# Gates of a recurrent attention kernel in two passes, and weight bits by ACT: one predicted change

## The chip, the cores and the metric

The kernel runs on one core of a Trainium2 chip. Time is the device time of one execution, in microseconds (us); the kernel before was run three times, with a median of 344.8 us (344.57 to 345.37). One further execution was recorded by the hardware profiler, and all rows of a trace come from it. The engines are PE (TensorE, matrix products, with its separate weight load PEld), DVE (VectorE), ACT (ScalarE), POOL (GpSimd) and SP (SyncE, which here only issues transfers). Each engine works through its own list of instructions in order, and waits where an instruction's operands are not there yet. ACT and POOL issue transfers too.

## The reference

The first part is a recurrent attention (an mLSTM) over 4 batches, 8 heads, 768 steps of 40 values. Each head keeps a matrix C and a vector n, and two gates per step, stabilized by a running maximum m:

```python
for t in range(S):
    m_new = np.maximum(f_gate[:, :, t] + m, i_gate[:, :, t])
    f_stab = np.exp(f_gate[:, :, t] + m - m_new)
    i_stab = np.exp(i_gate[:, :, t] - m_new)
    m = m_new
    C = f_stab[..., None, None] * C + i_stab[..., None, None] * (v_t outer k_t)
    n = f_stab[..., None] * n + i_stab[..., None] * k_t
    y[:, :, t] = sigmoid(o_gate[:, :, t]) * (C @ q_t) / max(abs(n . q_t), 1)
```

(The outer product and the dot products are written in short.) The second part takes y as x, 4 batches of 768 rows of 320: h = relu(x @ w_in) with 1024 columns is cut in u and v; v is normalized over its 512 columns; v_s = w_spatial @ v_n + b_spatial mixes the 768 rows of a batch; the output is (u * v_s) @ w_out. The weights w_in and w_out arrive as float64, all else as float32.

## The kernel before

**Blocks.** The recurrence is cut into 24 blocks n of 128 steps, six for each batch, all eight heads at once; a block has two chunks of 64 steps. A block's work is a chain over the engines:

- `s` on PE, the scores of the two chunks (L638); `ex` on PE (L641), which multiplies two small tables GM and AT and so gives the exponent of every gate weight; `W` on ACT (L656), its exponential; `KS` on DVE (L662), two products of scores and weights.
- `q` on POOL or DVE (L671), queries times the decay `Eb`. In the first batch Eb comes out of a product with `sel` (L651) and an exponential (L654); later batches load it from DRAM (L625).
- `kt` on POOL or DVE (L682), keys times weights in the tile RH; `dc` on PE (L693 for one chunk, L695 for the other), what each chunk adds to the state; the decays d1 and d2 of the state on POOL or DVE (L713, L723); the new states into RH on DVE (L716, L726), or for a batch's first chunk a copy.
- `pv` on PE (L737, L738), the outputs of scores and state; the denominators `den`, with ACT's part at L762 in the first batch, and `xm` (L753) and `xg` on DVE; the transposes `px` on PE (L786), and xH and xL, high and low halves of x.

Then `V` on PE (L839, tile pm) gives v of 128 rows, with its normalization on ACT, DVE and POOL; `pu` (L900) gives u; `pb` (L906 to L908) is the mixing over a batch's six blocks; g, gu, gh and gl on DVE and ACT make the gated product; `pc` (L950 to L952) is the output product, which is cast and stored. A float32 operand of these products is split into a high and a low part (H and L in the names) and three products of them are summed.

**Gates.** The gate rows are 32 (batch and head) by 768 steps. They are worked in three pieces, steps 0 to 128, 128 to 384 and 384 to 768: on DVE the running maximum m, a scan (L373), a difference (L380), its clipped negative (L383), a second scan that is reset at each chunk (L386) and a last difference (L389), for the two exponents g and a; then high parts on ACT (L407, L414) and low parts on DVE or POOL (L410, L417). The first piece goes by small transfers straight into GM and AT of block 0 (L447, L453). All pieces go into scratch in DRAM, from which SP loads each block's GM (L617) and each batch's AT (L464). ACT exponentiates g too (L428), and that scratch serves Eb.

**Weights.** w_in comes in five loads of float64 words and w_out in four. Each is turned into float32 by bits: ACT rebases the exponent of the upper word (L482, into wi_b or wir_b) and puts the sign into one byte in four of the tile sg (L486); DVE shifts the former left by three and joins the latter (L490), then joins the three top bits of the lower word (L493). A cast and a subtraction (L507) make the high and low parts.

**Order.** Two tables written out by hand set all of it: ORDER lists every task in the order in which it is emitted, for all engines together, and ENGINES names the engine of those tasks that have a choice. Two tasks joined by + are emitted in turns, instruction by instruction, as in `s2+dc1`. Tiles come from small pools, whose slots are reused in the order of the table.

Of the kernel before, what the change touches and what calls it, by code (L numbers as in the profile page):

```python
# [8 lines left out]
F32 = mybir.dt.float32  # L9
# [3 lines left out]
F8 = mybir.dt.float8e5  # L13
AF = mybir.ActivationFunctionType
# [22 lines left out]
PIECES = ((0, 128), (128, 384), (384, 768))  # L37
# [83 lines left out]
kt1 s2+dc1 d1_1 wi10_l0 ks1_1 q1_1 c1_1 qk3 wg0 wir_m0 gm4 wi01_0 W2 ko3 ra1 wir_m1 px0 wi01_1 xh0 ws04_l ws02_h pv1 eg2 wi01_2 ebm3 xl0 xj0 xk0 ks2_1
ws05_ld wir_m2 ex3 d2_1 q2_0 V00 gm5 ws02_l kt2 c2_1 ks2_0 da_1 Eb3 dp_1 xm1 xg1 we2 wi00_1 eg1 wi00_0 eg0 wi01_5 wi00_2 dc2+s3 W3 wi00_5 px1 d1_2
c1_2 re00 pv2 sq00 th2 ks3_1 wi01_h0 ws05_h xj1 q3_1 q3_0 d2_2 c2_2 ko4 kt3 d1_3 qk4 da_2 va00 wi01_l0 ks3_0 ex4 po00 dc3 c1_3 xh1 ebm4 Eb4 qk5 wo2_ld
ws05_l d2_3 dp_2 pv3 xk1 xm2 W4 kt4 xg2 xl1 ebm5 th3 da_3 ws00_ld c2_3 nb00 ex5 q4_0 dp_3 px2 xh2 Eb5 xj2 vn00 th4 W5 we0 gm6 xm3 xg3 xl2 s4 ks4_0
ks4_1 V01 dc4+s5 re01 ko5 sq01 px3 d1_4 xk2 c1_4 q4_1 pv4 ks5_0 wi00_h0 xh3 wo2_0 gm7 da_4 q5_0 ks5_1 q5_1 va01 dp_4 xj3 vh00 ws00_h d2_4 we1 c2_4 V02
re02 kt5 ex6 W6 xm4 ko6 d1_5 dc5 xg4 sq02 px4 ws00_l c1_5 po01 kt6 xh4 xj4 nb01 vh01 xk4 xl3 vl00 va02 po02 qk6 xl4 wi00_l0 vn01 pv5 eb7_0 eb6_0 qk7
da_5 dc6+s6 c1_6 th5 nb02 vn02 ko7 th6 vl01 eb7_1 V04 vh02 xk3 ks6_0 d2_6 re04 wir_z1 dp_5 V03 q6_1 q7_1 wo2_1 sq04 xm5 xg5 px5 ex7 s7 ws11_ld gm8
re03 ks6_1 wo2_2 va04 vl02 wo2_5 po04 pv6 W7 kt7 ks7_0 xj5 sq03 nb04 vn04 xh5 c2_6 vh04 xk5 xl5 q7_0 pu000 ex8 va03 ws03_ld ws11_h ws03_h vl04 po03
dc7 den6 ks7_1 V05 W8 ws01_ld d1_7 ws01_h qk8 nb03 vh03 ws15_ld ra2 qk9 ws01_l ws11_l c1_7 ws03_l re05 eb8_1 u000 ws13_ld gm9 pu001 sq05 va05 wo1_ld
ws15_h po05 vn03 u001 xm6 vl03 pv7 s8 nb05 s9 vh05 ex9 ws12_ld vn05 bsp eb8_0 vl05 xg6 ws15_l pb001 ko8 wo3_ld ws13_h gm10 W9 ks9_0 ws12_h ks8_0 wo1_0  # L130
wo2_h0 ws13_l wo1_1 wo1_2 pb003 gm11 d2_7 q8_1 wo2_l0 wo1_5 g001 den7 wo1_h0 wo3_0 wo3_1 ks9_1 wo0_ld wo1_l0 ko9 c2_7 ks8_1 pu003 g003 eb9_1 th7 u003
wo3_2 wo3_5 gu001 wo0_1 q8_0 ws12_l kt8 xm7 px6 xh6 d1_8 wo3_h0 gh001 xg7 wo3_l0 gu003 gl001 pu011 ws14_ld pb000 ws14_h u011 wo0_0 wo0_2 dc8 wo0_5 kt9
dc9 q9_0 c1_8 pu002 g000 gu000 ws14_l eb9_0 d2_8 pb002 ko10 wo0_h0 u002 ws10_ld c2_8 d1_9 pv8 c1_9 wo0_l0 g002 gh003 gl003 eb11_1 th8 q9_1 ws10_h pv9
xl6 gu002 ws10_l ex10 W10 d2_9 gh000 gh002 gl000 den8 qk11 kt10 pu010 pb011 eb10_0 gl002 g011 xm8 c2_9 den9 eb10_1 th10 d1_10 gm12 c02 qk10 oc02 gu011
eb11_0 xg8 c01 xm9 oc01 q10_0 c00 q11_0 u010 s10+dc10 ko11 xj6 ks10_1 xk6 oc00 th9 ks10_0 s11 px8 xh8 q10_1 c1_10 d2_10 pb010 ex11 xg9 ko12 pv10 q11_1
xl8 xj8 xk8 g010 px9 den10 xm10 eb12_0 gh011 W11 ex12 W12 qk12 pb013 xg10 px10 gu010 gh010 ks11_1 ks11_0 xh9 ko13 xh10 xl10 c2_10 pb012 pu012 u012 xj9
# [61 lines left out]
class Kernel:  # L198
# [155 lines left out]
    def gates(self):  # L354
# [7 lines left out]
        for z, (lo, hi) in enumerate(PIECES):  # L362
# [667 lines left out]
```

## Time and profile before

| what | value |
|---|---|
| median of three runs | 344.8 us (344.57 to 345.37) |
| the profiled execution's own time | 344.69 us |
| its span, first to last instruction | 342.9 us |
| PE busy | 321.5 us, 94% of the span |
| DVE busy | 243.1 us, 71% |
| ACT busy | 140.2 us, 41% |
| POOL busy | 140.0 us, 41% |
| DMA, mean | 123 GB/s |
| granted TensorE clock, mean | 0.999 |

The profile's page gives busy times, a picture of the span in 40 slices (each digit a busy share in tenths), groups of like instructions and a chain of waits. A row of the timeline gives the start in us from the span's start, the length in us, the engine, the line (L12 is line 12 of the kernel), the operation, output and inputs with their shapes, and in brackets how long the engine had been idle and what ended it. A row of a group gives the line, the count, busy us and mean ns of one, and after the second bar the idle time of the engine just before such instructions. A row of the waits gives who waited for what: us in all, how often, the longest.

### The profile page before, as it was taken

To read this page: it belongs to the slowest core of one execution; us is meant where nothing else is said; L and a number is where in the kernel's file an instruction comes from. 1 tells how busy PE (TensorE), PEld (TensorE's weight loads), DVE (VectorE), ACT (ScalarE), POOL (GpSimd) and SP (SyncE) were. 2 spreads that over 40 slices of the span, in tenths; PEclk is the share of its full clock that TensorE was granted. 3 is DMA by queue.
4 is the path that set the end of the run, shared out by engine and by line. 5 is a ranking of instruction groups with operands and counts; after the bars stand their busy time and mean duration, and the time that the engine had idled before them with its cause. 6 is when DMAs were issued, how large, how long until landed. Compare 5 with 4: busy or idle time off the path is not lost.

```text
span 342.9 us, 9048 instructions
## 1 busy us (share of the span) xinstructions
PE 321.5 (94%) x3654; PEld 296.0 (86%) x3654; DVE 243.1 (71%) x559; ACT 140.2 (41%) x327; POOL 140.0 (41%) x163
## 2 busy tenths in 40 slices
PE   2298899999999999999999999999999999999996
PEld 2177577898999989898999988999999889999995
DVE  4999999989856767857686677758838677325172
ACT  3769579844321159613113146740220187111001
POOL 6479898676444324561023227673300053100000
PEclk9999999999999999999999999999999999999999
DMA  8796877665343752324505522525210000100002
GB/s 244 253 328 188 248 236 239 165 226 171 121 119 112 233 150 90 106 73 142 175 30 175 181 62 87 175 65 182 98 38 2 3 0 21 38 0 21 19 21 76
DMA packets 17217, 42.13 MB, mean 123 GB/s; under 512 B 3572, under 2 KB 8664, under 8 KB 17176
## 3 DMA queue, kind: packets, MB, share of 16 engines
q1 hardware_dynamic: 11080, 24.31, 23.1%
q10 hardware_dynamic: 3872, 9.39, 8.2%
q0 software_dynamic: 2224, 7.86, 7.1%
q8 instruction: 29, 0.48, 0.6%
q14 instruction: 12, 0.10, 0.1%
HBM read 37.11 MB, written 4.42 MB: 121 GB/s over the span
## 4 chain that ended last, share of the span: by engine, by line
PE 79%; DVE 7%; ACT 4%; DMA 3%; POOL 3%; issue 2%; ACTq 0%; POOLq 0%; DVEq 0%
PE pu L900 13%; PE pm L839 12%; PE pb L906 9%; PE pb L908 9%; PE pb L907 9%; PE pv L737 5%; PE s L638 4%; PE pc L950 4%; PE pc L951 4%; PE pc L952 4%; PE px L786 2%; DMA ident<-in_ident 1%; POOL KS L671 1%; PE dc L693 1%; DMA ws<-in_w_sp 1%
## 5 line engine op out<-in xcount | busy, mean ns | idle before, releaser
L906 PE MATMUL pb<-wsH,vH 128*128 128x384 f32 x192 | 65.8, 342 | 0.0
L908 PE MATMUL pb<-wsH,vL 128*128 128x384 f32 x192 | 64.8, 338 | 0.0
L907 PE MATMUL pb<-wsL,vH 128*128 128x384 f32 x192 | 64.7, 337 | 0.0
L671 POOL TENSOR_TENSOR KS<-QK,Eb 40x512 f32<-40x512 f32 (+1 forms) x35 | 45.5, 1302 | 5.0 <-DMA QK<-in_qk 2.0
L662 DVE TENSOR_TENSOR KS<-s,W 64x512 f32<-64x512 f32 x48 | 32.9, 686 | 9.7 <-PE s L638 9.0
L924 DVE TENSOR_TENSOR pb<-pb,bsp 128x384 f32<-128x384 f32 x32 | 17.6, 560 | 26.9 <-PE pb L908 26.9
L638 PE MATMUL s<-QK 40*64 40x64 f32 x768 | 30.0, 233 | 6.7 <-DMA QK<-in_qk 6.2
L906 PEld LDWEIGHTS pb<-wsH,vH 128*128 128x128 f32 x192 | 36.1, 188 | 0.2
L907 PEld LDWEIGHTS pb<-wsL,vH 128*128 128x128 f32 x192 | 36.1, 188 | 0.1
L908 PEld LDWEIGHTS pb<-wsH,vL 128*128 128x128 f32 x192 | 36.0, 188 | 0.0
L638 PEld LDWEIGHTS s<-QK 40*64 40x64 f32 x768 | 27.0, 145 | 10.0 <-DMA QK<-in_qk 6.2
L723 POOL TENSOR_TENSOR tb<-RH,Eb 40x328 f32<-40x328 f32 x18 | 13.8, 768 | 52.6 <-DVE RH L716 28.3
L900 PE MATMUL pu<-xH,wiH 128*128 128x384 f32 x96 | 33.1, 345 | 0.4 <-DVE KS L662 0.4
L900 PE MATMUL pu<-xH,wiL 128*128 128x384 f32 x96 | 32.4, 338 | 0.0
L737 PEld LDWEIGHTS pv<-RH,KS 128*64 128x64 f32 x384 | 25.4, 145 | 7.9 <-issue 2.4
L737 PE MATMUL pv<-RH,KS 128*64 128x41 f32 x384 | 27.7, 237 | 3.7 <-DVE RH L716 2.4
L855 POOL TENSOR_TENSOR st<-st,half_neg 128x1 f32<-128x1 f32 x24 | 14.8, 618 | 39.8 <-DVE st L852 39.6
L839 PE MATMUL pm<-wiH,xH 128*128 128x512 f32 x72 | 30.3, 421 | 0.3 <-ACT W L656 0.3
L950 PE MATMUL pc<-woH,gt 128*128 128x320 f32 x96 | 29.9, 311 | 0.0
L951 PE MATMUL pc<-woL,gt 128*128 128x320 f32 x96 | 29.5, 308 | 0.0
L952 PE MATMUL pc<-woH,gt 128*128 128x320 f32 x96 | 29.5, 308 | 0.0
L839 PE MATMUL pm<-wiL,xH 128*128 128x512 f32 x72 | 29.1, 404 | 0.0
(133 smaller groups left out, 797.5 us busy)
## 6 DMA issues: line engine op xcount, KB each, us to landing
RH<-in_ko SPq DMA_DIRECT2D x12, 648.0 KB
QK<-in_qk SPq DMA_DIRECT2D x16, 448.0 KB
RH<-in_ko ACTq DMA_DIRECT2D x6, 648.0 KB
RH<-in_ko POOLq DMA_DIRECT2D x6, 648.0 KB, 5.5
Eb<-scr_e SPq DMA_DIRECT2D x33, 80.0 KB
ws<-in_w_sp SPq DMA_DIRECT2D x10, 192.0 KB
out<-o SPq DMA_DIRECT2D x12, 160.0 KB
out<-o ACTq DMA_DIRECT2D x12, 160.0 KB
```

What stands on the lines that cost most here:

```text
L638: yield self.nc.tensor.matmul(o[64 - p0:128 - p0, h], q[p0:p0 + D, 0, h], q[p0:p0 + D, 1, h], start=True, stop=True)
L662: self.nc.vector.tensor_tensor(out=KS.t[r, e], in0=st()[r], in1=self.T(W)[r], op=ALU.mult)
L671: self.on(f"q{n}_{e}", "POOL").tensor_tensor(out=KS.t[r, e], in0=self.T(QK)[r, 1], in1=self.T(Eb)[r], op=ALU.mult)
L737: self.nc.tensor.matmul(o[64:128, h], ks[:, 1, h], v1[:, h], start=True, stop=True)
L839: self.nc.tensor.matmul(pmt(), l, r, start=i == 0, stop=i == len(terms) - 1)
L900: self.nc.tensor.matmul(put(), w, x, start=i == 0, stop=i == len(terms) - 1)
L906: self.nc.tensor.matmul(pbt(), vH[:, cd], wh[:, s], start=s == 0, stop=False)
L907: self.nc.tensor.matmul(pbt(), vH[:, cd], wl[:, s], start=False, stop=False)
L908: self.nc.tensor.matmul(pbt(), vL[:, cd], wh[:, s], start=False, stop=s == NB - 1)
L950: self.nc.tensor.matmul(pct(), gH[:, c], wh[:, d], start=d == 0, stop=False)
L951: self.nc.tensor.matmul(pct(), gH[:, c], wl[:, d], start=False, stop=False)
L952: self.nc.tensor.matmul(pct(), gL[:, c], wh[:, d], start=False, stop=d == 3)
```

## The change

**Gates.** The first pass takes steps 0 to 128 on 32 rows, as before. Then one scan of the maximum covers the other 640 steps. Four differences of 192 steps each then put the four quarters of the sequence onto four groups of 32 partitions, so that all 128 partitions hold 192 steps; the clipped negative, the reset scan, the last difference, the high and low parts and the exponential are done once on 128 by 192. This second pass computes the first block's steps again, for the scratch. The scratch is laid out by quarters: a load of Eb takes 40 partitions by 8 heads in runs of 64 values from 8 places, where its source was one run of 512. There is one write each to the scratch of g, a and Eb where there were three. The order of the rows of g in GM changes, and the constants atr and sel with it.

**Weights.** The low bits are no longer joined by DVE at L493. ACT reads the top byte of the lower word as an integer from 0 to 255, multiplies it by 7.49/255 and stores it, as an integer from 0 to 7, into another byte of sg. The shift then joins sign and low bits at once.

**Tables.** ORDER and ENGINES are new throughout; the diff shows their first lines only. The pairs joined by + were `s2+dc1 dc2+s3 dc4+s5 dc6+s6 s10+dc10 s12+dc11 s13+dc13 dc14+s15 dc15+s16 s17+dc17 s18+dc18 s19+dc19 s20+dc20 s21+dc21 s22+dc23 s23+dc22` and are now `dc2+s3 s5+dc5 s7+dc7 s11+dc10 dc11+s12 s13+dc13 dc14+s15 s16+dc16 s17+dc17 s19+dc19 s21+dc20 s23+dc23 s22+dc22`. From the scores on, line numbers are two higher (L638 is L640).

```diff
-PIECES = ((0, 128), (128, 384), (384, 768))
...
 ORDER = """
-gmr1 sgz rst half_neg f gmr0 i ident m0 is0 atr0 fs0 g0 as0 wi11_ld qk0 msk sel wir_ld wir_z0 ko0 atc0 gh0 atr1 dg0 ah0 atc1 wi11_0 gl0 al0 m1 is1 dg3
-da0 dg1 fs1 g1 wa0 as1 wi11_1 dg2 s0 da1 gh1 gmc0 m2 wi11_2 gl1 wir_1 wg1 ex0 is2 fs2 ah1 wir_0 wi10_ld al1 qk1 W0 wir_2 ebm0 Eb0 ko1 kt0 gmc1 th0 dc0
...
+atr0 wir_z0 msk sgz i f rst gmr1 ident wi11_ld m0 is0 qk0 fs0 g0 as0 wir_ld gmc0 gmc1 gh0 gl0 sel dg2 ah0 al0 ko0 dg3 wi11_1 wi11_5 atc0 da1 s0 m1 nd2
+nd1 nd0 nd3 fs1 g1 as1 gmr0 dg0 wi11_0 wi10_ld ko1 dg1 gh1 da0 qk1 ah1 wir_1 gl1 wi11_2 wi01_ld ex0 W0 wir_5 ws05_ld ebm0 Eb0 al1 wir_0 wg kt0 ks0_1
+ks0_0 wir_2 wa dc0 wi10_1 wi10_5 wi10_0 qz_0 q0_1 c1_0 pv0 da_0 gm2 gm1 ra0 wi10_2 ebm1 d2_0 ebm2 ex1 c2_0 dp_0 qk2 ws02_ld atr1 th0 wi10_h0 Eb1 ex2
...
-        self.scr_g = dram.tile([BH, NB, 4, L], F32, name="scr_g")
-        self.scr_e = dram.tile([2 * NB, BH, L], F32, name="scr_e")
-        self.scr_a = dram.tile([BH, 2, S], F32, name="scr_a")
+        self.scr_g = dram.tile([BH, 4, NB // 2, 2, L], F32, name="scr_g")
+        self.scr_e = dram.tile([BH, 4, NB // 2, L], F32, name="scr_e")
+        self.scr_a = dram.tile([BH, 4, 2, S // 4], F32, name="scr_a")
...
 
     def gates(self):
...
-        for z, (lo, hi) in enumerate(PIECES):
...
-                self.nc.vector.tensor_tensor_scan(out=p[:, s:hi], data0=i[:, s - 1:hi - 1], data1=f[:, s:hi], initial=first, op0=ALU.max, op1=ALU.add)
...
-            add(f"fs{z}", "DVE", dve(n), fstab, r=[(ft, P)], w=[(eg, P)])
...
+        add("m0", "DVE", 0.5, lambda: scan_p(0, 128), r=[(ft, 0), (it, 0)], w=[(mt, 0)], lock=True)
+        add("m1", "DVE", 0.14 + 2.2 * 640 / 960.0, lambda: scan_p(128, S), r=[(ft, 1), (it, 0), (it, 1), (mt, 0)], w=[(mt, 1)], lock=True)
...
+        SEG = S // 4
+        for z in range(2):
...
+                for q in range(4):
+                    def diff(q=q):
+                        c = slice(q * SEG, (q + 1) * SEG)
+                        self.nc.vector.tensor_tensor(out=self.T(sg)[q * BH:(q + 1) * BH, 0:SEG], in0=T(it)[:, c], in1=T(mt)[:, c], op=ALU.subtract)
...
+            def fstab(A=A, Bf=Bf):
+                self.nc.vector.tensor_scalar(out=Bf(), in0=A(), scalar1=-1.0, scalar2=0.0, op0=ALU.mult, op1=ALU.min)
...
+            def scan_g(Bf=Bf, C=C, rows=rows, n=n):
+                self.nc.vector.tensor_tensor_scan(out=C(), data0=F("rst").t[0:rows, 0:n], data1=Bf(), initial=0.0, op0=ALU.mult, op1=ALU.add)
...
+            def a_sub(A=A, C=C):
+                self.nc.vector.scalar_tensor_tensor(out=A(), in0=A(), scalar=0.0, in1=C(), op0=ALU.min, op1=ALU.subtract)
...
+            add("wg", "SP", 0.4, lambda: self.dma("SP")(out=self.scr_g.rearrange("b s j w t -> s b (j w t)"), in_=half(0)), r=parts[0], w=[F("scr_g")], size=8)
+            add("wa", "SP", 0.4, lambda: self.dma("SP")(out=self.scr_a.rearrange("b s w x -> s b (w x)"), in_=half(1)), r=parts[1], w=[F("scr_a")], size=8)
+            add("eg", "ACT", 0.4 + n / 1200.0, lambda: self.nc.scalar.activation(out=Bf(), in_=C(), func=AF.Exp), r=[kc], w=[kb], due=25.0)
+            add("we", "SP", 0.35, lambda: self.dma("SP")(out=self.scr_e.rearrange("b s j t -> s b (j t)"), in_=Bf()), r=[kb], w=[F("scr_e")], size=8, due=29.0)
...
+    def load_a(self, b):
+
+        AT = self.F(f"AT{b % 2}")
+
+        def load():
+            return self.nc.sync.dma_start(
+                out=AT.t[68:84].bitcast(F32).rearrange("r (s x) -> r s x", s=4), in_=self.scr_a[b * H:(b + 1) * H].rearrange("h s w x -> w h s x"))
+        self.add(f"ra{b}", "SP", 0.6, load, r=[self.F("scr_a")], w=[(AT, ("a", z, w)) for z in range(2) for w in range(2)], size=16)
...
         def low():
-            self.nc.vector.scalar_tensor_tensor(out=bt(), in0=W()[:, :, 0], scalar=29, in1=bt(), op0=ALU.logical_shift_right, op1=ALU.bitwise_or)
+
+            self.nc.scalar.activation(
+                out=sg.t[:, 0:n].bitcast(U8).rearrange("p (n w) -> p n w", w=4)[:, :, 0], in_=top(),
+                func=AF.Copy, scale=7.49 / 255.0)
+
+        def top():
+            return self.T(rb, [128, 2 * n], F32).bitcast(U8).rearrange("p (n w) -> p n w", w=8)[:, :, 3]
 
         add(name + "_ld", "SP", 0.45, load, w=[rb], size=n, alt=LOADS)
         add(name + "_1", "ACT", c_act, rebase, r=[rb], w=[bits])
-        add(name + "_0", "ACT", c_act, sign, r=[rb], w=[signs], after=self.sgz)
+        add(name + "_0", "ACT", c_act, sign, r=[rb], w=[(signs, 0)], after=self.sgz)
+        add(name + "_5", "ACT", c_act + 0.16, low, r=[rb], w=[(signs, 1)], after=self.sgz)
         add(name + "_2", "DVE", c_dve, shift, r=[signs], w=[bits])
-        add(name + "_5", "DVE", c_dve, low, r=[rb], w=[bits])
...
-                        out=self.T(Eb)[64 * e:64 * e + D], in_=self.scr_e[2 * k + e, b * H:(b + 1) * H].unsqueeze(0).broadcast_to([D, H, L]))
+                        out=self.T(Eb)[64 * e:64 * e + D], in_=self.scr_e.rearrange("b s j t -> b (s j) t")[b * H:(b + 1) * H, 2 * k + 1 - e].unsqueeze(0).broadcast_to([D, H, L]))
...
-    r["atr"] = (np.arange(4)[:, None] % 2 == s[None] // L).astype(np.float32)
+    r["atr"] = (np.arange(4)[:, None] // 2 == s[None] // L).astype(np.float32)
```

**The first instructions of ACT.** Before, the cast of the identity into AT (tile AT_76) stands ahead of the high parts of the first block's g and a (gp_130, ap_134):

```order
L274 ACT_TABLE_LOAD
L274 CAST AT_76<-ident 64x768
L407 CAST gp_130<-gc 32x128
L414 CAST ap_134<-ft 32x128
L274 CAST AT_78<-ident 64x768
L486 ACTIVATE sg<-wi_raw 128x512
L482 ACTIVATE wi_b<-wi_raw 128x512
```

In the change (both high parts are in px_126; L476 is the rebase, L488 the low bits, L480 the sign):

```order
L274 ACT_TABLE_LOAD
L274 CAST GM_75<-msk 64x512
L274 CAST GM_77<-msk 64x512
L418 CAST px_126<-zt 32x128
L424 CAST px_126<-ft 32x128
L606 DMA RH_88<-in_ko 128x1296
L476 ACTIVATE wi_b<-wi_raw 128x512
L488 ACTIVATE sg<-wi_raw 128x512
L274 CAST AT_76<-ident 64x768
L480 ACTIVATE sg<-wi_raw 128x512
```

Two casts of the mask into the GM tiles now stand ahead of the high parts; the identity's cast comes later, among the three ACT operations of the first weight piece.

**DVE around block 0's KS.** Before, with the third gate piece (32x384) among the first weight operations:

```order
L373 SCALAR_TENSOR_TENSOR mt<-it,mt,ft 32x384
L490 SCALAR_TENSOR_TENSOR wi_b<-wi_b,sg 128x512
L410 TENSOR_TENSOR gp_170<-gc,gp_170 32x2x128
L380 TENSOR_TENSOR ft<-it,mt 32x384
L383 TENSOR_SCALAR eg<-ft 32x384
L417 TENSOR_TENSOR ap_183<-ft,ap_183 32x256
L490 SCALAR_TENSOR_TENSOR wir_b<-wir_b,sg 128x512
L662 TENSOR_TENSOR KS_87<-s_152,W_191 64x512 x2
L493 SCALAR_TENSOR_TENSOR wi_b<-wi_raw,wi_b 128x512
L493 SCALAR_TENSOR_TENSOR wir_b<-wir_raw,wir_b 128x512
L386 SCALAR_TENSOR_TENSOR gc<-rst,eg 32x384
L389 SCALAR_TENSOR_TENSOR ft<-ft,gc 32x384
```

In the change (sg_158 is the tile of the four quarters, px_173 its high and low parts, L684 is kt, L484 the shift):

```order
L369 SCALAR_TENSOR_TENSOR mt<-it,mt,ft 32x640
L398 TENSOR_TENSOR sg_158<-it,mt 32x192 x4
L405 TENSOR_SCALAR sg_158<-sg_158 128x192
L408 SCALAR_TENSOR_TENSOR sg_158<-rst,sg_158 128x192
L411 SCALAR_TENSOR_TENSOR sg_158<-sg_158 128x192
L484 SCALAR_TENSOR_TENSOR wi_b<-wi_b,sg 128x512
L427 TENSOR_TENSOR px_173<-sg_158,px_173 128x192
L684 TENSOR_TENSOR RH_88<-RH_88,W_187 128x320
L664 TENSOR_TENSOR KS_87<-s_140,W_187 64x512 x2
L484 SCALAR_TENSOR_TENSOR wir_b<-wir_b,sg 128x512
L274 COPY RH_88<-dc_204 40x328
```

The third piece and the low-bit rows are gone; kt of block 0 and the copy of its state are now on DVE.

**PE at block 21's state products.** Before, dc_3247 stood in turns with the scores s_3245 of the same block:

```order
L638 MATMUL s_3245<-QK_3088 64x64
L693 MATMUL dc_3247<-RH_88 40x41
L638 MATMUL s_3245<-QK_3088 64x64
L695 MATMUL dc_3247<-RH_88 40x41
L638 MATMUL s_3245<-QK_3088 64x64
```

In the change dc_3381, the same work, follows the products of a pu:

```order
L902 MATMUL pu_3368<-xL_2356,wiH 128x384
L902 MATMUL pu_3368<-xH_2146,wiH 128x384
L902 MATMUL pu_3368<-xH_2146,wiL 128x384
L695 MATMUL dc_3381<-RH_88 40x41
L697 MATMUL dc_3381<-RH_88 40x41
```

It stands alone there, its two lines in turns with each other only.

More of the change, by code (lines that the diff above doesn't have):

```diff
@@ L13 @@
 F8 = mybir.dt.float8e5
+U8 = mybir.dt.uint8
 AF = mybir.ActivationFunctionType
@@ new lines @@
+    ("ACT", """wi10_ld wi11_ld wi00_ld wi01_ld ws00_ld wo2_ld ws12_ld ko0 ko1 ko2 qk4 qk5 ko10 qk10 qk11 ko12 ko13 qk13 ko16 ko17 ko18 qk20 ko21 ko22 ko23
+        vn10 vn13 vn15 vn20 vn21 vn22 vn25"""),
+    ("DVE", """wi11_h0 wir_h0 wir_m3 ws02_h ws03_l ws11_h ws13_h ws14_h kt0 c1_0 xh0 q2_0 xj6 q7_0 xj7 xh8 xj8 xh10 xj10 xj11 kt12 c1_12 xj12 q13_1 q14_1
+        kt14 xh14 xj14 xh15 xj15 q16_0 xj16 q17_1 xj17 q18_1 xh18 kt19 q20_1 xh20 xj21 kt22 xj22 xj23 vl01 vl02 vn03 vl04 vn05 vl05 u002 oc02 u011
+        gh011 oc04 oc05 vl11 vl15 u100 gh101 u102 gh102 oc11 u110 gh111 gh113 vl23 vl25 u200 u201 gh202 oc20 oc22 gh213 oc23 oc24 vl35 u300 u302
+        oc31 gh310 u312 u313 gh313"""),
@@ L121 @@
[L121 to L124, printed above, removed]
@@ L451, in gates @@
+                    add(f"dg{r}", "SP", 0.6, d_g, r=[(pp, ("g", r % 2))], w=[(F("GM0"), ("g", r))], size=1, alt=(("ACT", 0.5, 0), ("POOL", 0.55, 0)))
                 for w in range(2):
-                    def d_a(w=w, apt=apt):
-                        self.on(f"da{w}", "ACT").dma_start(out=F("AT0").t[68 + 8 * w:76 + 8 * w, 0:128].bitcast(F32), in_=apt()[0:H, w].bitcast(F32))
-                    add(f"da{w}", "ACT", 0.5, d_a, r=[(ap, w)], w=[(F("AT0"), ("a", 0, w))], size=1, alt=(("SP", 0.6, 0), ("POOL", 0.55, 0)))
@@ new lines, in gates @@
+                    add(f"da{w}", "ACT", 0.5, d_a, r=[(pp, ("a", w))], w=[(F("AT0"), ("a", 0, w))], size=1, alt=(("SP", 0.6, 0), ("POOL", 0.55, 0)))
+                continue
+            half = lambda j, P=P: P()[:, 2 * j:2 * j + 2].rearrange("p r x -> p (r x)").bitcast(F32)
+            parts = [(pp, ("g", 0)), (pp, ("g", 1))], [(pp, ("a", 0)), (pp, ("a", 1))]
+            add("wg", "SP", 0.4, lambda: self.dma("SP")(out=self.scr_g.rearrange("b s j w t -> s b (j w t)"), in_=half(0)), r=parts[0], w=[F("scr_g")], size=8)
@@ L613, in attention @@
         if k == 0 and b:
-            add(f"ra{b}", "SP", 0.6, lambda: self.read_a(b, 0, S), r=[F("scr_a")], w=[(AT, ("a", zz, w)) for zz in range(3) for w in range(2)], size=16)
+            self.load_a(b)
+        if n == 1:
+            self.load_a(0)
         if n:
```

230 lines of the change are left out of this document (101 added, 129 removed).

## The prediction

> **What bounds the kernel now.** I read the page first, for busy shares and their place in the span, then the windows by stage, then the waits and the timeline of the first 30 us.
>
> ```profile
> span 342.9 us, 9048 instructions
> PE   2298899999999999999999999999999999999996
> DVE  4999999989856767857686677758838677325172
> ```
>
> ```profile
> 0.00:30.00 30.00, 15.41 (x229) 12.26 (x230) 23.76 (x47) 19.16 (x38) 19.91 (x32) 1.00 0.78 250
> 30.00:60.00 30.00, 28.08 (x473) 21.48 (x470) 27.66 (x63) 23.50 (x64) 26.18 (x29) 1.00 0.81 246
> 60.00:72.00 12.00, 12.00 (x221) 10.65 (x221) 10.53 (x27) 9.31 (x22) 8.37 (x10) 1.00 0.66 195
> 72.00:340.00 268.00, 265.97 (x2740) 251.62 (x2738) 181.14 (x426) 88.01 (x206) 85.57 (x94) 1.00 0.29 92
> ```
>
> The columns are the stretch, its length, then PE, PEld, DVE, ACT and POOL busy, the granted clock, the DMA share and GB/s. Two stages with different limits are seen. From 72 us on PE is busy 265.97 of 268.00 us: what happens on DVE there costs nothing, and only PE's own list sets the time. Before that PE waits: 14.6 of the first 30 us and 1.9 of the next. DVE is the full engine there, 27.66 of 30 us in the second stretch, and 23.76 of the first 30 although it starts late:
>
> ```profile
> PE pv L737 <- DVE RH L716: 2.2, 5, 1.1
> 3.87 0.41 DVE L373 TENSOR_TENSOR_SCAN mt<-it,ft 32x127 f32<-32x127 f32 x1 [2.47 <-DMA it<-in_i_gate]
> 27.92 0.49 DVE L716 TENSOR_TENSOR RH<-dc,ta 40x328 f32<-40x328 f32 x1
> 28.56 0.30 PE L737 MATMUL pv<-RH,KS 128*64 128x41 f32 x1 [1.09 <-DVE RH L716]
> ```
>
> PE's matmul pv, one per block, waited five times in the first 60 us for the state update RH on DVE (L716). That update is not slow, 0.49 us; it stands at the end of a full queue. So the first 72 us go by the length of DVE's list, the rest by PE's. The change shortens the first and, as the order shows, slightly lengthens the second.
>
> At the end nothing is touched: the last output cast starts at 339.59 and its transfer closes the span at 342.9; in the changed order a last product, a cast on ACT and a transfer close it too. I take 0, with 0.3 us either way, the length of one casting row.
>
> ```profile
> 339.59 0.42 ACT L274 COPY o<-pc 128x320 f32<-128x320 f32 x1 [1.28 <-PE pc L952]
> ```
>
> **The first block's gates: about 1 us earlier.**
>
> ```profile
> 5.33 0.41 DVE L386 TENSOR_TENSOR_SCAN gc<-rst,eg 32x128 f32<-32x128 f32 x1
> 6.34 0.83 ACT L274 CAST AT<-ident 64x768 fp32r<-64x768 f32 x1 [2.42 <-DMA ident<-in_ident]
> 7.08 0.29 ACT L407 CAST gp<-gc 32x128 fp32r<-32x128 f32 x1
> 9.70 0.66 SPq L453 DMA_DIRECT2D AT<-ap  x1
> 13.12 0.77 PE L641 MATMUL ex<-GM,AT 84*128 84x512 f32 x1 [4.97 <-DMA wi_raw<-in_w_in]
> 13.94 0.58 ACT L656 ACTIVATE W<-ex 128x512 f32<-128x512 f32 x1
> 16.68 0.52 POOL L707 MEMSET KS<- 40x512 f32 x1
> 17.33 0.41 PE L737 MATMUL pv<-RH,KS 128*64 128x41 f32 x2 [0.57 <-POOL KS L707]
> ```
>
> The scan ends at 5.74, but ACT's split of it (L407) starts only at 7.08, behind the cast AT that waited for the identity. In the change two casts of the mask stand there, and the identity's cast comes later; the mask is a smaller transfer, issued first on SP. The split then starts near 5.9, 1.2 us earlier. On SP the small DMAs into GM and AT follow each other at about 0.7 us; before, the last began at 9.70 behind a write to DRAM that is gone. With four in a row from about 6.2 the last begins near 8.3, and ex, which came 3.42 us after that DMA (13.12 - 9.70), near 11.8. I take 11.9: 1.2 us earlier. Against it: f now follows the mask on SP, which may cost up to 0.7 us (one issue), since DVE started when both gates had landed.
>
> The first pv waited for a memset on POOL behind two products. In the change the memset precedes them, and the chain is W on ACT (1.4 us after ex by its rows), then on DVE kt (L682, below, with KS, L662, and the shift, priced as L493), two KS, one shift and the copy of the state, priced as the RH above: 0.58 + 2 x 0.69 + 0.69 + 0.49 = 3.1. 11.9 + 1.4 + 3.1 = 16.4 against 17.33: 0.9 us.
>
> **DVE's list up to the second block's pv.**
>
> ```profile
> L373 DVE TENSOR_TENSOR_SCAN mt<-it,mt,ft 32x256 f32<-32x256 f32 (+1 forms) x2 | 1.7, 866 | 0.0
> L386 DVE TENSOR_TENSOR_SCAN gc<-rst,eg 32x128 f32<-32x128 f32 (+2 forms) x3 | 2.0, 674 | 0.1
> L380 DVE TENSOR_TENSOR ft<-it,mt 32x127 f32<-32x127 f32 (+2 forms) x3 | 1.2, 409 | 0.1
> L383 DVE TENSOR_SCALAR eg<-ft 32x128 f32<-32x128 f32 (+2 forms) x3 | 1.2, 408 | 0.1
> L389 DVE SCALAR_TENSOR_TENSOR ft<-ft,gc 32x128 f32<-32x128 f32 (+2 forms) x3 | 1.2, 412 | 0.1
> L410 DVE TENSOR_TENSOR gp<-gc,gp 32x128 fp32r<-32x128 f32 (+1 forms) x2 | 0.7, 340 | 1.4 <-ACT gp L407 1.4
> L417 DVE TENSOR_TENSOR ap<-ft,ap 32x128 fp32r<-32x128 f32 (+1 forms) x2 | 0.7, 341 | 0.3 <-ACT ap L414 0.3
> L493 DVE SCALAR_TENSOR_TENSOR wi_b<-wi_raw,wi_b 128x512 int32<-128x512 int32 x4 | 2.8, 689 | 0.1
> L662 DVE TENSOR_TENSOR KS<-s,W 64x512 f32<-64x512 f32 x48 | 32.9, 686 | 9.7 <-PE s L638 9.0
> L682 DVE TENSOR_TENSOR RH<-RH,W 128x320 f32<-128x320 f32 x8 | 4.6, 575 | 0.0
> L753 DVE TENSOR_TENSOR pv<-pv,den 128x320 f32<-128x320 f32 x24 | 11.9, 494 | 0.7
> L486 ACT ACTIVATE sg<-wi_raw 128x512 fp8e5<-128x512 f32 x4 | 3.1, 774 | 0.3 <-DMA wi_raw<-in_w_in 0.2
> L482 ACT ACTIVATE wi_b<-wi_raw 128x512 f32<-128x512 f32 x4 | 2.5, 627 | 0.0
> ```
>
> Removed: the gate rows of three pieces (scans 0.4 + 1.7 + 2.0, three element-wise groups of 1.2, low parts 0.7 + 0.7: 9.1 us), and five low-bit operations of 0.69 = 3.4 us, three of them before this pv. Added: a first pass at the old 128-wide price (2.0 us), one scan over 640 and four differences over 192, and a pass over 192 on all 128 rows. No row shows these. The scan cost 0.41 at 127 and, by the mean 866 of the 256 and 384 forms, 0.87 at about 320, so 640 lies between 0.9 (no growth) and 1.7 (the same growth); I take 1.6, on the line. A difference of 192 lies between 0.28 and 0.41, the 127 form and the group's mean; I take 0.35, four are 1.4. The pass over 192, five instructions, 1.9. Sum 6.9: 2.2 us saved on gates, 2.1 on the three low operations. Other work moved onto DVE before this pv: the state copy, kt, three weight casts and one of xH, minus one each of wiL and a decay moved off: about +2.1. The list up to the RH before this pv, 21.7 us by the groups' durations, becomes 21.7 - 2.2 - 2.1 + 2.1 = 19.5.
>
> Walking it from 16.4: the shift wi_b and one RH (1.2), then DVE waits for pv's 2.0 us and ACT's small den, to 18.6; den, pv, x, three wiH and wiL operations, KS, a move, KS, xH, wiL, a wsH cast and RH are 7.6 us at 0.69 for 512 elements, 0.5 for 320 and 0.4 for the small ones: 26.2, and pv at 26.3 against 28.56. The lead has grown from 0.9 to 2.3 us. Its bounds: 0, if ACT makes DVE wait for all of it (below), and 3.3, if the 4.3 us that leave the list count in full and half of the 2.1 that came finds idle time.
>
> **From there to 72 us.** The two orders, each row at its group's mean duration, give DVE 42.2 us before and 41.7 now, and ACT 41.6 and 41.7: the low operations of the last two weight pieces and of w_out on ACT are paid there by three-piece exponentials that became one. I give this stretch 0.2 us, half the difference. The low operation itself has no row: its nearest is the sign's, which also writes one byte in four, 774 ns (627 for a full store); I take 0.78.
>
> **PE's list: 1.4 us more.** The program has the same matmuls, but state products dc are often issued between the score products s of another block, on other rows of the array.
>
> ```profile
> 85.10:86.46 1.36, 1.36 (x64) 1.31 (x64) 0.00 (x0) 0.00 (x0) 1.00 0.83 198
> 103.50:104.48 0.98, 0.97 (x32) 0.91 (x32) 0.00 (x0) 0.00 (x0) 1.00 0.00 0
> 103.50:104.48 0.98, 0.98 (x32) 0.98 (x34) 0.00 (x0) 1.00 0.00 0
> ```
>
> The first row has only dc: two groups alone took 1.36 us, 0.68 each. The other two are one stretch, seen for dc and for s: 32 of each in 0.98 us, so a paired dc costs nothing beside s. After 72 us four dc stand alone before (blocks 8, 9, 12, 16) and six in the change (8, 9, 12, 15, 18, 21): 2 x 0.68 = 1.4 us where PE has no idle time. Its bounds are 0, if they fall into stalls, and 1.5. Before 72 us the solo groups change places, and PE has room.
>
> **Hidden.** The scratch for the decays is now laid out by quarters of the sequence, so each load Eb reads 256 bytes at a time where it read 2 KB. I cost it at nothing: POOL, which uses Eb, is busy 85.57 of 268 us and DMA engines 0.29 of that stretch. Without the cover, an Eb that lands 0.5 us late delays one pv by as much. The Trainium skill, "DMA: Bandwidth & Descriptors", section "Specifications", speaks against the change here: it names 512 bytes as the smallest transfer at line rate. By it these loads would cost more DMA time, and the sum stays, since the share is 0.29. w_out's four low operations leave DVE where PE bounds.
>
> **Sum.** The profiled execution took 344.69 us, 342.9 of span and 1.8 around it; the runs' median is 344.8. 344.69 - 2.3 - 0.2 + 1.4 + 0 = 343.6, and 0.1 for the median: **343.7 us**.
>
> **Rivals.** *ACT's low operation blocks DVE's queue.* Each shift (L490) now waits for three ACT operations instead of two; behind it on DVE stand the KS or state copy for which PE waits. My walk has the second low operation done 0.2 us before DVE asks, and the third after it. From the point where ACT is later than DVE at all of the first three conversions, DVE loses 3 x 0.78 = 2.3 us, the whole lead, and the two solo dc remain: 344.8 - 0.2 + 1.4 = 346.0, slower. For it: ACT is busy 23.50 of 30 us from 30 on. Against it: 6 us idle there, and 11 in the first 30.
>
> *Transfers bound the start.* DMA engines are busy 0.78 and 0.81 in the first 60 us. If the weights cannot come earlier, the lead stays near 0.9, the first block's: 344.8 - 0.9 + 1.4 = 345.3, no change. For it that share; against it that most waits shown are for engines.
>
> *The slow matmuls end earlier.*
>
> ```profile
> 31.44 0.63 PE L839 MATMUL pm<-wiH,xH 128*128 128x512 f32 x1
> 31.87 0.63 PE L839 MATMUL pm<-wiL,xH 128*128 128x512 f32 x1
> 55.33 3.97 PE pm L839 x16
> ```
>
> The first group of pm runs at 0.43 us a matmul, later ones at 3.97 / 16 = 0.25, with the granted clock at 1.00 in both. If PE, fed more densely, reaches the fast pace before this group, its eight matmuls save 8 x 0.18 = 1.4 us more: 342.3. The change leaves a wait before the second pv, as now, so I do not count on it. The Trainium skill, "TensorE: Matmul & The Clock Gate", section "What's actually happening", tells the same: half rate until some 3.4 us of sustained work. The trace agrees in the factor; the place of the switch is open.
>
> *The new order has fewer late stalls.* PE's 2.0 idle us after 72 could vanish: 341.7. No row speaks for it.
>
> **Chances.** Forecast 0.48 (its own range 342.6 to 345.0), ACT blocks 0.17, transfers 0.13, earlier fast pace 0.14, fewer stalls 0.08. About 0.2%, 0.7 us, is what a measurement can tell from no change: faster is below 344.1, slower above 345.5. Faster: 0.7 of the forecast and the last two, 0.56. Same: the rest of the forecast, but a little, and most of the transfers, 0.23. Slower 0.21. The range 341.3 to 346.1 takes in all but the tails of both sides.
>
> **What would show it.** Right: ex of the first block near 11.9, the second pv near 26.3, no L493 on DVE, PE full before 70 us, and the solo dc of blocks 15, 18 and 21 at 0.68 us each. Wrong: DVE shifts with idle time released by ACT sg; the second pv at 28 or later; PE waiting after 72 us for POOL's products with Eb; the first pm group at 0.25 us.

## The result, and the profile after

The change made the kernel slower, by 1.5%: 350.3 us median (349.61 to 351.14) against 345.09 for the kernel before in the same comparison, a ratio of 1.015 (95% interval 1.0114 to 1.0186). The forecast was 343.7 and its range ended at 346.1. The profiled execution of the change took 349.68 us. Medians here and below are of all executions, while the ratios leave out single executions in a slower state of the chip, such as two of the ten of one run below. Its page and its windows, with the columns as above:

```profile
span 347.9 us, 9026 instructions
PE   0449899999999999999999999999999999999995
DVE  5476999879776586876684767567666377425062
```

```profile
0.00:30.00 30.00, 11.49 (x139) 8.53 (x139) 15.67 (x34) 16.52 (x30) 13.61 (x26) 1.00 0.77 242
30.00:60.00 30.00, 28.52 (x515) 23.41 (x515) 28.09 (x66) 23.41 (x59) 27.57 (x30) 1.00 0.72 226
60.00:72.00 12.00, 12.00 (x192) 10.05 (x192) 9.94 (x23) 10.85 (x27) 7.90 (x11) 1.00 0.62 180
72.00:340.00 268.00, 266.15 (x2793) 251.77 (x2790) 173.52 (x413) 93.95 (x219) 91.17 (x99) 1.00 0.31 94
```

The loss is in the first row. PE did 11.49 us of work in the first 30 where it had done 15.41, and DVE, whose list was to set the pace, fell from 23.76 to 15.67: both waited. The timelines give the start of some of PE's groups:

| us | before | change |
|---|---|---|
| ex of block 0 | 13.12 | 15.05 |
| ex of block 1 | 20.31 | 26.12 |
| pv of block 1 | 28.56 | 33.63 |
| first pb | 71.72 | 75.15 |
| end of the last product | 339.55 | 344.34 |

So 3.43 us were lost up to the first pb, and 1.36 from there to the last product (269.19 against 267.83); from that to the end of the span it is 3.56 against 3.35. The sum, 5.0, is the difference of the spans. The four longest waits of PE in the first 60 us of the change (who waits for what: us, times, longest):

```profile
PE s L640 <- DMA QK<-in_qk: 9.7, 1, 9.7
PE ex L643 <- DMA AT<-px: 3.4, 1, 3.4
PE eb L653 <- DMA GM<-scr_g: 2.0, 1, 2.0
PE ex L643 <- DMA AT<-scr_a: 1.5, 1, 1.5
```

The first is the start, before any product; it ends 5.4 us ahead of ex of block 0. The other three are transfers of gate tables: the direct ones of block 0, and for blocks 1 and 2 the scratch in DRAM. The chain of waits of the change up to there (start, length, what):

```profile
6.25 6.89 DMA RH<-in_ko
13.21 8.87 DMA scr_a<-px
22.15 3.84 DMA AT<-scr_a
26.12 1.19 PE ex L643 x2
```

The second gate pass had its results by 11.94 (the low part, L427, starts at 11.58 and takes 0.36). From then on the chain is transfers alone: the write of a takes 8.87 us from its issue, the read into AT 3.84. Not all of the 8.87 is slow moving: the trace's records of single DMA packets have the first scratch row at 16.63, so that 3.4 us went by before anything of either write moved. The windows of the change around that write:

```profile
12.00:16.00 4.00, 0.95 (x2) 0.50 (x2) 0.00 (x0) 0.14 (x1) 0.80 (x2) 1.00 1.02 308
16.00:18.00 2.00, 1.21 (x29) 0.97 (x30) 1.47 (x3) 2.00 (x4) 0.36 (x1) 1.00 0.80 303
19.00:21.00 2.00, 1.46 (x28) 1.49 (x30) 0.93 (x3) 1.40 (x2) 1.52 (x3) 1.00 0.27 101
```

Up to 16 us the DMA engines are full with weights, keys and queries. But between 19 and 21, when little beside the scratch writes is under way, they are busy to 0.27, as much as some four engines of 16, and move 101 GB/s, a third of the 308 of the first row. Two writes of 128 rows each, of g and of a, take until 20.2 and 22.1 us while most engines rest.

### The profile page after: what moved, and what is told of

It reads as the page before. It is cut to its first block, busy times and chain, and to the rows that moved or that the text cites. A ratio compares the mean times of both kernels' runs of the same rounds, so it can differ in the third digit from the quotient of the medians.

```text
span 347.9 us, 9026 instructions
## 1 busy us (share of the span) xinstructions
PE 322.5 (93%) x3654; PEld 297.8 (86%) x3654; DVE 228.6 (66%) x535; ACT 146.3 (42%) x336; POOL 140.3 (40%) x163
## 4 chain that ended last, share of the span: by engine, by line
PE 84%; DMA 6%; ACT 3%; DVE 3%; POOL 1%; issue 1%; SPq 0%; ACTq 0%; POOLq 0%; DVEq 0%
PE pu L902 13%; PE pm L841 12%; PE pb L908 10%; PE pb L910 10%; PE pb L909 10%; PE pv L739 5%; PE s L640 4%; PE pc L952 4%; PE pc L953 4%; PE pc L954 4%; DMA scr_a<-px 3%; PE dc L695 2%; DMA RH<-in_ko 2%; PE px L788 2%; PE ex L643 1%; DMA AT<-scr_a 1%
## 5 line engine op out<-in xcount | busy, mean ns | idle before, releaser
L673 POOL TENSOR_TENSOR KS<-QK,Eb 40x512 f32<-40x512 f32 (+1 forms) x36 | 46.9, 1308 | 19.6 <-ACT Eb L656 8.5
L640 PE MATMUL s<-QK 40*64 40x64 f32 x768 | 29.8, 233 | 10.0 <-DMA QK<-in_qk 9.7
L640 PEld LDWEIGHTS s<-QK 40*64 40x64 f32 x768 | 27.0, 145 | 13.1 <-DMA QK<-in_qk 9.7
L919 ACT ACTIVATE u<-pu 128x384 f32<-128x384 f32 x21 | 10.3, 493 | 56.5 <-PE pu L902 56.5
L857 POOL TENSOR_TENSOR st<-st,half_neg 128x1 f32<-128x1 f32 x24 | 13.6, 566 | 43.4 <-DVE st L854 42.7
```

Source lines behind the costliest of these rows:

```text
L640: yield self.nc.tensor.matmul(o[64 - p0:128 - p0, h], q[p0:p0 + D, 0, h], q[p0:p0 + D, 1, h], start=True, stop=True)
L673: self.on(f"q{n}_{e}", "POOL").tensor_tensor(out=KS.t[r, e], in0=self.T(QK)[r, 1], in1=self.T(Eb)[r], op=ALU.mult)
```

## The experiments

Two theories were set against each other first. The order table puts large loads ahead of the small gate transfers, which then have to share the DMA engines with them (theory 1); or the scratch write is slow by its own form (theory 2). A third, from the prediction, was that ACT's low bits hold up DVE. Each ratio is against the kernel before in the same comparison.

**Loads later.**

```diff
-... dg0 wi11_0 wi10_ld ko1 dg1 gh1 da0 qk1 ah1 ... wi01_ld ex0 W0 wir_5 ws05_ld ...
+... dg0 wi11_0 dg1 gh1 da0 qk1 ah1 wi10_ld ... ex0 W0 ko1 ... wa ws05_ld ... wi10_0 wi01_ld ...
```

> The change with five loads moved back in the order: w_in's fourth piece (ACT) behind the high parts of the second gate pass, QK of block 1 behind the direct transfers into AT, ko of block 1 behind block 0's W, w_in's fifth piece behind the three ACT operations of the fourth, and one piece of w_spatial behind the scratch writes. Theory 1, the small gate transfers are slow because large loads were put ahead of them on the other queues: ex of block 0 goes from 15.05 to about 13, the scratch write of a lands near 19 instead of 22.1, ex of block 1 starts near 23 instead of 26.1, and the time falls by 2 to 3 us to about 347.5. Theory 2, the scratch write itself is slow, whatever runs beside it: ex of block 0 improves alike, ex of block 1 stays within 1 us of 26, time within 1 us of 350.3. The weights then come later, and V of the first rows may become the wait: against 1 us of the gain.

351.2 us, ratio 1.0159 (1.0086 to 1.0231): nothing gained. Block 0 gained as theory 1 says, ex at 13.61, but ex of block 1 came at 26.51. The chain:

```profile
12.35 10.33 DMA scr_a<-px
22.76 3.62 DMA AT<-scr_a
```

The write was issued 0.86 us earlier and landed no earlier. This alone does not clear the loads: those that were moved back now ran beside the write (the engines were busy to 0.74 from 18 to 20 us). (The load of QK stood already where the expectation puts it; the other four moved.)

**Scratch with the quarter outermost.**

```diff
-        self.scr_a = dram.tile([BH, 4, 2, S // 4], F32, name="scr_a")
+        self.scr_a = dram.tile([4, BH, 2, S // 4], F32, name="scr_a")
...
-out=self.scr_a.rearrange("b s w x -> s b (w x)")
+out=self.scr_a.rearrange("s b w x -> (s b) (w x)")
```

(The same for g and e; AT is read in two transfers, one for each half, and GM of two blocks in six too.)

> The change with the three scratch tensors laid out with the quarter outermost, so that each write is one contiguous run of 128 rows; the table loads of two blocks in six and the load of AT then take two transfers each. Theory 2 (a write whose outer dimension is 4 moves at only 98 to 104 GB/s with nothing beside it, as between 18 and 21 us): the write of a lands near 18.5 instead of 22.1, ex of block 1 starts near 23 instead of 26.1, time 347 to 348. Theory 1 (company of large loads): the write starts at 16.6 as before and lands no earlier than 20.5; time within 1 us of 350.3.

347.35 us, ratio 1.0041 (1.0009 to 1.0074), beside 1.015 for the change. Its windows and chain:

```profile
16.00:18.00 2.00, 1.21 (x33) 1.13 (x32) 1.63 (x3) 2.00 (x5) 0.52 (x1) 1.00 0.99 376
19.00:21.00 2.00, 1.61 (x31) 1.64 (x32) 0.93 (x2) 1.29 (x2) 1.67 (x3) 1.00 0.09 25
```

```profile
13.04 7.34 DMA scr_a<-px
20.77 2.76 DMA AT<-scr_a
```

The engines are full to 18 us and nearly idle from 19 (0.09); the write's end is signalled at 20.38 (13.04 + 7.34), 1.7 us earlier than in the change. ex of block 1 starts at 23.66 and the first pb at 72.70, 2.45 us earlier than in the change. Theory 2 is borne out; part of the gain is the read, now in two transfers, which landed 2.76 us after the second was issued (3.84 in the change).

**Rows apart.** The layout had changed two things, the outer dimension of the write and whether its rows touch in DRAM.

```diff
-        self.scr_a = dram.tile([4, BH, 2, S // 4], F32, name="scr_a")
+        self.scr_a = dram.tile([4, BH, 400], F32, name="scr_a")   # 384 used
```

> The change with the spread scratch for g and a, but with each of the 128 rows padded from 384 to 400 values, so that a write has 128 rows and no two of them touch in DRAM. If the number of outer rows is what makes the write of the change slow (4 there, 128 here): as with the spread scratch, ex of block 1 near 23.7 and about 347.4. If it is that the written places are apart in DRAM: ex of block 1 near 26 and about 350.3.

347.9 us, ratio 1.0059 (1.0023 to 1.0095), ex of block 1 at 23.96. With 128 rows that don't touch, the engines were as full:

```profile
16.00:18.00 2.00, 1.22 (x14) 0.49 (x15) 0.89 (x2) 1.55 (x3) 0.00 (x0) 1.00 1.01 388
```

So it is the outer dimension, 4 in the change and 128 here. The trace's records of completions show it more directly. A transfer has a counter (a semaphore) that is raised as it lands: for the write of a by four updates in the change, between 21.31 and 22.07 us, and by sixteen here, between 18.70 and 19.55. The Trainium skill, "DMA: Bandwidth & Descriptors", section "Why a DMA increments its semaphore by 16 and not by 1", states this rule: a transfer runs on the largest number of engines, up to 16, that divides the outermost dimension of both its sides. By it the write gets four engines, and the 0.27 of the trace agrees.

**Four writes.** The change's layout, each scratch write as four transfers of 32 rows:

```diff
+for q in range(4): dma(out=scr_a[:, q].rearrange("b w x -> b (w x)"), in_=half(1)[q * BH:(q + 1) * BH])
```

> The change with its scratch layout kept, but each of the three scratch writes split into four transfers, one for each quarter, of 32 rows each. The bytes, the rows and their places in DRAM are the same; only the outer dimension of a transfer goes from 4 to 32. If the small outer dimension is what makes the one write slow (few DMA engines share it): the DMA share between 18 and 21 us is no longer near 0.3 with writes alone under way, the read of AT starts 1 to 2.5 us before 22.15 in spite of six more issues of about 0.55 us on SP, and the time falls by 1 to 2.5 us from 350.3. If the strided places in DRAM are what makes it slow: the read starts at 22 us or later, the issues cost up to 3 us on SP, and the time is 350 to 353.

349.51 us, ratio 1.0101 (1.0067 to 1.0136): by the time alone inconclusive. The last write took 1.52 us, but SP could issue it only at 19.75, since it waited for loads to land (its waits, and the chain):

```profile
SPq L448 <- DMA RH<-in_ko: 2.9, 1, 2.9
SPq L448 <- DMA wi_raw<-in_w_in: 0.9, 1, 0.9
```

```profile
19.75 1.52 DMA scr_a<-px
21.34 4.64 DMA AT<-scr_a
```

These waits are the program's own: in the trace each such issue waits on the counter that its transfer will use, and a load still under way counts on the same one. The writes themselves agree with the rule. Each raises its counter by sixteen updates, and with scratch rows most of what moves the engines are busy to 0.52, twice the 0.27 of the change:

```profile
18.50:19.50 1.00, 0.14 (x5) 0.00 (x0) 1.00 (x3) 0.68 (x3) 0.70 (x1) 1.00 0.52 158
```

**Both edits.** Spread scratch and later loads together.

> Both edits together. If each of the two causes is real, ex of block 0 near 13, ex of block 1 near 21, and the time near 345.5, the sum of the two gains; if one of them is all of it, this equals the better of the two single edits within 0.7 us.

346.87 us, ratio 1.0039 (1.0008 to 1.0071): no better than the spread scratch alone within the intervals. Its trace has ex of blocks 0 and 1 at 13.87 and 22.59 and the first pb at 71.84, level with 71.72 before: in this execution all but 0.12 us of the loss at the start is gone, and none of the gain that was forecast has come. What else is left of its span over that of before, 344.6 against 342.9, is PE's list: 269.41 us from the first pb to the last product, 267.83 before.

**Low bits back on DVE**, in the changed order:

```diff
-        add(name + "_5", "ACT", c_act + 0.16, low, r=[rb], w=[(signs, 1)], after=self.sgz)
+        add(name + "_5", "DVE", c_dve, low, r=[rb], w=[bits])
```

> The change with the low bits back on DVE (one shift-and-or over 512 columns behind the first, as before the change), the order otherwise kept but for one load of w_out. If ACT's low operation holds up DVE's shifts in the first blocks: faster than the change by 1 us or more. If the first blocks go by transfers, as the waits of the changed kernel say: ex of block 1 stays at 26 us, DVE has 3.4 us more work, some of it between 33 and 60 us where DVE is full, and the time is the same or up to 1.5 us slower, 350 to 352.

350.61 us, ratio 1.0139 (1.0087 to 1.0192): the same as the change. DVE's 3.4 us are not on the path there.

**Low bits on ACT alone**, in the order of before:

> The kernel before with one part of the change alone: the low bits by ACT, in the order of before, each ACT operation put just ahead of its shift. Theory A (in the kernel before the first 60 us go by DVE's list, as the prediction read it): three operations of 0.69 us leave that list ahead of the second pv, which comes 1 to 2 us earlier than 28.56, and the time falls by 1 to 2 us against 345.1. Theory B (ACT, which gets 0.78 us for each 0.69, holds up the shifts, or the wait moves on to a transfer): second pv within 0.5 us of 28.56 or later, time within 0.7 us of before, or slower.

345.12 us, ratio 1.0002 (0.9971 to 1.0033): nothing that can be measured. The profiled execution, at 343.14 the fastest of its four, has the second pv at 26.89, as theory A says, but DVE waits for ACT's low bits (L494):

```profile
DVE wi_b L490 <- ACT sg L494: 1.7, 2, 1.5
DVE wir_b L490 <- ACT sg L494: 1.4, 1, 1.4
```

**The gates alone**, in the order of before (the third piece's tasks gone, `is1` replaced by `nd0 nd1 nd2 nd3`, `wg1 wa1` by `wg wa`):

> The kernel before with the other part alone: the gates in two passes and the scratch by quarters as in the change, the low bits on DVE, order and engines of before (the third piece's tasks left out, the four differences where the second piece's was). If the write with four outer runs is the cause: ex of block 1 moves from 20.31 to between 22 and 24, since it now waits for the transfers, which takes back the 2.2 us that DVE saves; time from the same to 1.5 us slower than 345.1. If the cause was only the place of the loads in the changed order, ex of block 1 stays within 0.7 us of 20.31 and the time falls by 1 to 2 us.

350.5 us, ratio 1.0177 (1.0132 to 1.0222), as slow as the whole change, with its order and engines left out. The chain:

```profile
13.59 7.47 DMA scr_a<-px
21.14 7.74 DMA AT<-scr_a
```

ex of block 1 starts at 29.02, 8.7 us later than before and 5 later than expected at most: the read into AT took 7.74 us as well, with the DMA engines busy to 0.97 around it (21 to 29 us). So the gates bring the loss without the new order table and the low bits.

**With the spread scratch**:

> The same with the scratch laid out quarter outermost, so that a write is one run of 128 rows. If the write's form is the cause: ex of block 1 back within 0.7 us of 20.31, the second pv 1 to 2 us earlier than 28.56, time 343 to 344. If not: as the run without it.

346.95 us, ratio 1.0065 (1.0031 to 1.0099). ex of block 1 is back at 20.41, but another transfer took its place, the queries of block 2, which stood on SP behind the scratch read:

```profile
26.84 0.34 PE L642 MATMUL s<-QK 40*64 40x64 f32 x1 [3.18 <-DMA QK<-in_qk]
```

**And with that load issued by ACT** (`qk2` in ACT's list):

> The kernel before with the two-pass gates, the spread scratch, and one more edit: the load of QK for block 2 is issued by ACT, where it stood on SP behind the read of AT from the scratch. In the run without this edit (346.95) the scores of block 2 waited until 26.84 for that load, issued at 17.60. If that queue is all that is left of the cost: the scores of block 2 start near 24, the second pv near 28, and the time is 344 to 345, no slower than before. If the load waits for other traffic wherever it is issued: scores of block 2 near 26 to 27, time 346.5 to 347.5.

344.8 us, ratio 0.9997 (0.9967 to 1.0028): level with before. Scores of block 2 start at 23.62, the second pv at 27.04. The 6 us of the gates were, by the medians, 3.5 for the form of the scratch (its writes and its reads changed together) and 2.2 for the load behind it; once both are gone, the DVE work saved shows as nothing in them. The profiled execution, which took 343.72 us, has the first pb at 70.52, 1.2 us ahead of before; the medians don't confirm it.

**Adding the low bits on ACT** to these two:

> The order of before with both parts of the change and the spread scratch. If the two parts each save DVE time where DVE sets the pace: 3 to 4 us less DVE work ahead of the second pv, time 341.5 to 343. If DVE's list stops being the bound after the first of them (ACT or transfers next): within 0.7 us of the better single part.

> The same with the low bits on ACT too. If DVE's list is the bound once the transfers are out of the way, this is 1 to 2 us faster than the run with gates alone, and faster than before (343 to 344). If transfers or ACT still hold the first blocks: within 0.7 us of it, or slower.

348.23 us (1.0103, 1.0075 to 1.0131) and 348.5 us (1.0118, 1.0034 to 1.0202): slower. In the second DVE waits for ACT's low bits (L489), and the read into AT takes 6.70 us (waits of DVE; chain):

```profile
DVE wi_b L485 <- ACT sg L489: 2.8, 2, 1.5
DVE wir_b L485 <- ACT sg L489: 1.4, 1, 1.4
```

```profile
14.24 4.79 DMA scr_a<-px
19.41 6.70 DMA AT<-scr_a
```

Which of the two costs more was not told apart.

**PE's lone products.** Five pairs of before taken apart (`s17+dc17` to `s21+dc21` become `s17 dc17` and so on):

> The kernel before with five pairs taken apart: the scores of blocks 17 to 21 first, then their state products dc alone; nothing else moved. If a dc alone costs PE 0.68 us where it has no idle time, and nothing when paired: 5 x 0.68 = 3.4 us slower than before, all of it after 150 us, about 348. If PE's order there is not the bound or the pairs save less: under 1.5 us slower.

346.88 us, ratio 1.0025 (0.9987 to 1.0064), which doesn't tell it from before. The traces do, from the first pb to the last product, before and then with the pairs apart:

```profile
71.72:339.55 267.83, 266.25 (x2741) 251.89 (x2739) 181.42 (x426) 87.67 (x205) 85.57 (x94) 1.00 0.29 92
```

```profile
71.51:341.31 269.80, 268.22 (x2741) 253.98 (x2739) 182.12 (x426) 87.67 (x205) 85.21 (x94) 1.00 0.29 92
```

1.97 us for five, 0.39 each and not 0.68: a lone dc right behind its own scores overlaps them, and the two take 1.50 us (182.13 to 183.63) where the pair took 1.15. **Pairing again** what the change left alone, on top of both edits:

> The change with the spread scratch and the later loads (346.87 with both), and two of its three lone state products in PE's full stage paired with scores again: s18 with dc18, s20 with dc20 and s21 with dc21 in place of s21 with dc20. Two lone dc less are 1.36 us by the sum of the prediction: 345.5, and the stretch from the first mixing product (pb) to the last product back from 269.4 to about 268.0. If the lone products are not what the changed order costs in that stage: 346.9.

351.56 us, ratio 1.0131 (1.0068 to 1.0194). PE waits in the stage that was full, 5.6 us in all, and the granted clock is lower:

```profile
72.00:340.00 268.00, 262.39 (x2700) 247.47 (x2700) 170.35 (x405) 91.83 (x216) 88.91 (x96) 0.99 0.30 90
```

The waits are new where the pairs were put: PE is idle 2.20 us between 190 and 220 and 2.23 between 220 and 250, in the run that this builds on 0.00 and 0.64. That the pairs' operands were not ready there is likely but was not followed up; either way this says nothing on the price of a lone product.

## Why the prediction was wrong

**What bounds the kernel.** That two stages have different limits held. The step that failed is "So the first 72 us go by the length of DVE's list". It was read from PE's five waits for RH, and from a busy DVE; the transfers behind the gates had slack in the kernel before (ex of block 1 followed eb with no wait), and the working had no term for them once they changed. The change makes one write out of three, gives it four engines, and lets blocks 1 and 2 wait for it: where the sum has 2.3 and 0.2 us gained up to the first pb, 3.43 were lost.

**The first block's gates.** The split did start at 5.93, as forecast (near 5.9). The step that failed here is "ex, which came 3.42 us after that DMA": the last small transfer into AT was issued at 8.68, near the 8.3 forecast, but ex came only 6.4 us after that, at 15.05. Rows of the change's timeline show what had been put ahead of it:

```profile
6.74 0.33 ACTq L472 DMA_DIRECT2D wi_raw<-in_w_in  x1
7.10 0.72 ACTq L606 DMA_DIRECT2D RH<-in_ko  x1
7.93 1.39 SPq L442 DMA_DIRECT2D AT<-px  x2
```

Before, the keys of block 1 were issued at 14.36. With the loads later, ex came at 13.61 and 13.87. That is 1.2 to 1.4 of the 3.15 us between 11.9 and 15.05; what held the small transfers for the rest stays open.

**DVE's list.** The prices were right:

```profile
L369 DVE TENSOR_TENSOR_SCAN mt<-it,mt,ft 32x640 f32<-32x640 f32 x1 | 1.5, 1532 | 0.0
L398 DVE TENSOR_TENSOR sg<-it,mt 32x192 f32<-32x192 f32 x4 | 1.4, 348 | 0.1
```

1.53 us for the scan (1.6 forecast) and 1.4 for the differences (1.4); DVE was busy 228.6 us in all, 243.1 before. What failed is the step that walks this list from the first pv to the second as if DVE had its operands: the second pv, forecast at 26.3, came at 33.63. DVE stood idle twice for the late tables, once behind ex of block 0 and W, and once behind the scores of block 1, which the order puts after ex of block 1:

```profile
DVE RH L684 <- ACT W L658: 4.5, 1, 4.5
DVE KS L664 <- PE s L640: 4.1, 1, 4.1
```

Some of the saving is seen behind the second pv: from there to the first pb the change took 41.52 us, the kernel before 43.16, though 0.9 of these 1.6 are PE's pace (below).

**ACT.** The low operation took 0.77 us (0.78 forecast). In the changed order DVE waited 1.1 us in all for ACT's last of three, there the sign (L480), and taking the low bits back to DVE gained nothing. That rival fell for this order; in the order of before its waits are real, 3.1 us with the low bits alone, though the time did not change.

**PE's list** was the one term that came out: 1.4 forecast, 1.36 measured, all of it busy time (267.61 against 266.25; idle 1.58 in both):

```profile
75.15:344.34 269.19, 267.61 (x2740) 253.39 (x2740) 172.75 (x409) 93.50 (x219) 89.25 (x96) 1.00 0.30 91
```

The three lone dc that it named, of blocks 15, 18 and 21, are there, each taking PE 0.74 us until its next product starts (0.68 forecast; the rows are for dc only):

```profile
151.80:152.54 0.74, 0.74 (x34) 0.69 (x32) 0.00 (x0) 0.00 (x0) 1.00 0.77 243
201.35:202.10 0.75, 0.75 (x32) 0.70 (x32) 0.00 (x0) 0.00 (x0) 1.00 0.57 145
244.42:245.16 0.74, 0.74 (x32) 0.69 (x32) 0.00 (x0) 0.00 (x0) 1.00 0.12 28
```

The price does not hold in every place: right behind its own scores a lone dc costs 0.39. What the rest of the new order costs or saves PE was not measured apart.

**Eb** in runs of 256 bytes cost nothing, as forecast: with the gates alone, in the same order as before, that stretch (first pb to last product) took 267.23 us against 267.83, and none of PE's waits after 72 us in the change is for POOL's products with Eb.

**The rivals.** "Transfers bound the start" was the right mechanism, with a chance of 0.13 and a wrong price: it kept the first block's lead of 0.9 us and let transfers only hide a gain. They took 3.4 us more. The fast pace did come earlier in part: the first pm group took 2.62 us, where it took 3.54 before.

## What to carry to other kernels

When a change merges several small transfers into one, price the one by its outer dimension, by what is queued ahead of it and by who is first to wait for it: here 384 KB written in two transfers on four engines cost more than all of the arithmetic saved. A busy engine with waits behind it is the bound only as long as the transfers beside it keep their slack; write their landing times into the walk too. An order that puts large loads ahead can delay small transfers on other queues: with four loads moved back, ex of block 0 came at 13.61 instead of 15.05. And look at which counter an issue waits on: a program that reuses one can hold a small write until a large load has landed.

## What the runs showed of the hardware

As a transfer of SP lands, its counter is raised by several updates, and their number went with the transfer's form: four for the write with an outer dimension of 4, sixteen for one of 32 or 128 rows, two for the change's read into AT, whose source has an outer dimension of 2. SP's waits for a load of another queue (L448 for RH, 0.8 us in the change, 2.9 with four writes) come from the program: the trace shows an instruction of SP that waits on the counter of that load.

PE's pace in the first pm group varied from 2.62 to 3.55 us with the granted clock at 1.00 throughout; in the change it turned from 0.43 to 0.23 us a matmul near 38.0 us, in the kernel before at the group's end near 35.0, though PE had waited less. The Trainium skill, "TensorE: Matmul & The Clock Gate", section "What's actually happening", has the turn in a window that runs free of the kernel; that fits, and no run here tests it.
